# One Trainium2 core, attention into a mixture of experts: first attention's values three units behind its scores, k through VectorE, two weight words converted ahead of chunk 1

## The chip, the cores and the metric

The kernel runs on one core of a Trainium2 chip. TensorE (PE) multiplies matrices, with its weight loads shown apart as PEld; VectorE (DVE), ScalarE (ACT) and GpSimd (POOL) work element by element; SyncE (SP) issues the DMAs. Each engine takes its own instructions strictly in the order in which they are written and waits on semaphores for the others. The metric is the device time of one execution in microseconds (us), as the median of three runs.

## The reference

```
scores = q @ k.T / 8                      # 4 batches, 8 heads, 576 positions, 64 wide
mask: heads 0-3 the last 32 positions; heads 4-7 every 4th of the last 128
attn = exp(scores - max) / (sum + 1e-9);  x = attn @ v   -> 2304 tokens x 512
h = x @ w_in;  x = (h - tanh(h)) @ w_out                 # 512 -> 2048 -> 512
logits = x @ phi                                         # 8 experts x 4 slots
slots  = softmax over tokens(logits).T @ x
slots  = relu(slots[e] @ w1[e]) @ w2[e]  for 8 experts
out    = softmax over slots(logits) @ slots
```

## The kernel before

The mask lets most scores fall away, so the attention of a batch is worked in 12 units, three for each of the four head pairs (in the order `PO`): units 0 to 5 are dilated heads, in 4 blocks of 80 columns, units 6 to 11 are plain ones, in 3 blocks of 96. A unit goes round the engines:

1. **scores** (`emit_scores`): TensorE lays the mask into PSUM (L337) and adds the scores (L359); VectorE takes the largest (L374); ScalarE takes the exponentials and their sums (L377); VectorE adds the epsilon (L389) and inverts (L391); 
2. **norm** (`emit_norm`): GpSimd multiplies by the inverse (L392);
3. **trans** (`emit_trans`): TensorE transposes the weights (L401); ScalarE copies them out of PSUM (L103, `COPY mem<-mm`);
4. **values** (`emit_pv`): TensorE multiplies by v (L422); ScalarE casts the result to its high part (L103, `CAST xhi<-mm`);
5. **low** (`emit_lows`): VectorE subtracts to get the low part (L458).

For each head pair q and k are transposed by TensorE (L308) and taken out of PSUM as `qk` tiles of 128x288: k by a plain copy (L103), q by L316 with the factor 1/8. L103 is the line of the helper `copy`, which runs on the engine that it is told.

The 2048 columns of the hidden layer are 16 **words** of 128 columns. The weights arrive as raw words and are turned into the operands of three fp32r products: `conv_a` (ScalarE, L507), `conv_b` (two VectorE instructions, L515 and L516), then `conv_in_c` (a cast, L103 `CAST wts<-cvb` or `wts<-mem`, and GpSimd's low part, L529). `conv_out_c`, `_d` and `_e` (TensorE L537, L548, L561 and copies by L103) fold the output weights with phi. `emit_h` computes one word for 512 tokens: 4 parts of 3 matmuls (L574 to L576, high by high, low by high, high by low); then tanh (ScalarE, L580), h - tanh h (VectorE, L583) and the logits (L589).

The tokens go in chunks of 512. The order of the program is that of three stages:

- The **first attention** (batch 0) is emitted from a table: `at(t, f, ...)` puts each step of each unit, each conversion and each load at a model time, and the steps are emitted in the order of these times. A unit is 3.45 model us (`ATT0`); `NORM`, `TRANS` and `PV` say how far behind the unit's scores its other steps stand. The weights of words 1 and 2 (`conv_*("in", 0)` and `1`) are converted within it; `emit_h(..., part=range(3))` computes the first three of the four parts of words 1 and 2 at its end (the high parts, as they are called here: "high part 0" and "high part 1"). `warm` matmuls (L205) fill TensorE.
- **Chunk 0** (called chunk 1 where chunks are counted from one) runs as eight **mixed steps** s = 0 to 7 (`mixed_step`), each with words a = 2s and b = 2s + 1, a piece of the attention of batch 1 (`norms`, `trans`, `score`, `values`; masked on VectorE by L371), and the conversions of two words of input and two of output weights for later steps.
- The other chunks run as `phase_step`s, whose weights are all there, then experts and output.

Of the kernel before, what the change touches and what calls it, by code (L numbers as in the profile page):

```python
# [36 lines left out]
    ("out", 0): 0, ("out", 2): 1, ("out", 4): 2, ("in", 0): 3, ("in", 2): 0, ("in", 4): 1, ("out", 6): 2, ("in", 6): 3,  # L37
    ("out", 8): 2, ("out", 10): 1, ("in", 8): 2, ("in", 10): 3, ("out", 14): 2, ("in", 14): 3,
}
ENGS = {'qk': 'AAAA', 'pt': 'AAA', 'hi': 'AAA', 'rem': 'VVA', 'wh': 'VA', 'wt': 'AV', 'wq': 'V', 'wp': 'A'}  # L40
WARM = 5
NWARM = 4
WAT = 0.29
ATT0 = (8.71, 3.45)
NORM = (1.01, 0.28)
TRANS = (2.05, 1.76)
PV = (2.8, 3.39)
QK = (1.54, 1.08)
LQK = (12.33, 21.85)
LV = (4.31, 7.03)  # L50
# [9 lines left out]
LWI = 2.97  # L60
# [4 lines left out]
def moe_kernel(ctx: ExitStack, tc: tile.TileContext, q, k, v, w_in, w_out, phi, w1, w2, out):  # L65
# [8 lines left out]
    NU = 3 * NP  # L74
# [81 lines left out]
    wp = cpart(NFT, NS)  # L156
# [4 lines left out]
    wts, xhi, xlo = {}, {}, {}  # L161
# [340 lines left out]
    def conv_a(kind, ft):  # L502

        f = convs[kind].next()
        hw = raw_t[kind, ft][1].bitcast(F32)

        nc.scalar.activation(out=like(f, kind), in_=hw, func=ACTF.Prelu, scale=2.0 ** -112, alpha=-2.0 ** 32)  # L507
        cvt[kind, ft] = f

    def conv_b(kind, ft):  # L510
        wl, _ = raw_t.pop((kind, ft))
        f = cvt[kind, ft]
        du = f.bitcast(U32)
        dk = like(f, kind).bitcast(U32)
        nc.vector.tensor_scalar(out=du, in0=du, scalar1=3, scalar2=None, op0=ALU.logical_shift_left)  # L515
        nc.vector.scalar_tensor_tensor(  # L516
            out=dk, in0=wl, scalar=29, in1=dk, op0=ALU.logical_shift_right, op1=ALU.bitwise_or
        )
# [4 lines left out]
    def conv_in_c(ft):  # L523
        if ft % 2 == 0:
            wts[ft // 2] = unit("wts", [128, 2, KT, 256], F32R)
        fv = cvt.pop(("in", ft)).rearrange("p (k f) -> p k f", k=KT)
        hi, lo = win(0, ft), win(1, ft)
        copy(ENGS["wh"][ft > 1], hi, fv)
        nc.gpsimd.tensor_tensor(out=lo, in0=fv, in1=hi.bitcast(F32), op=ALU.subtract)  # L529
# [37 lines left out]
    def emit_h(xh, xl, ft, ps=None, part=range(KT)):  # L567

        if ps is None:
            ps = ps_h.tile([128, 512], F32, tag="h", name="h")[:, 0:xh.shape[-1]]  # L570
        for n in part:
            kt = PO[n]
            wh, wl = win(0, ft)[:, kt, :], win(1, ft)[:, kt, :]
            nc.tensor.matmul(ps, lhsT=wh, rhs=xh[:, kt, :], start=(n == 0), stop=False)  # L574
            nc.tensor.matmul(ps, lhsT=wh, rhs=xl[:, kt, :], start=False, stop=False)  # L575
            nc.tensor.matmul(ps, lhsT=wl, rhs=xh[:, kt, :], start=False, stop=(n == KT - 1))  # L576
        return ps

    def emit_tanh(ps, g):
        nc.scalar.activation(out=g, in_=ps, func=ACTF.Tanh)  # L580

    def emit_sub(ps, g):
        nc.vector.tensor_tensor(out=g, in0=ps, in1=g, op=ALU.subtract)  # L583
# [295 lines left out]
    with tc.manual_schedule():  # L879
# [4 lines left out]
        def at(t, f, *args):  # L884
            steps.append((t, len(steps), f, args))

        for b, (t0, dt) in enumerate((ATT0,)):
            for i in range(NU):
                t = t0 + dt * i
                at(t, emit_scores, b, i)  # L890
                at(t + 0.02 * dt, emit_lows)
                at(t + NORM[b] * dt, emit_norm, b, i)
                at(t + TRANS[b] * dt, emit_trans, b, i)
                at(t + PV[b] * dt, emit_pv, b, i)
                if b == 0:
                    at(t + WAT * dt, warm, WARM if i < NWARM else 2)
            for i in range(NU, NU + 3):
                at(t0 + dt * (i + 0.02), emit_lows)
            for p in range(NP):
                for n in range(2):  # L900
                    at(t0 - 0.02 + 0.01 * n if p == 0 else t0 + dt * (3 * p - 3 + n + QK[b]), emit_qk, b, PO[p], n)
                at(t0 + dt * 3 * p - LQK[b], load_qk, b, PO[p])
                at(t0 + dt * 3 * p - LV[b], load_v, b, PO[p], nc.sync)
# [4 lines left out]
        for e in range(KA):  # L908
            t, dt = WO1[0] + WO1[1] * e, WO1[1]
# [3 lines left out]
            at(t + OC * dt, conv_out_c, e)  # L913
            at(t + OD * dt, conv_out_d, e)
            at(t + OE * dt, conv_out_e, e)
        for e in range(2):
            t, dt = WI[0] + WI[1] * e, WI[1]
            at(t - LWI, load_w, "in", e)
            at(t, conv_a, "in", e)
            at(t + CB, conv_b, "in", e)  # L920
            at(t + IC * dt, conv_in_c, e)
        at(45.0, load_w, "in", 2)
        first = []
        for i in range(2):

            at(ATT0[0] + ATT0[1] * (10.65 + 0.5 * i + PV[0]), lambda i: first.append(emit_h(xhi[0], xlo[0], i, part=range(3))), i)
        at(WI[0] + 6.0, scale_q, 1, PO[0])
        for _, _, f, args in sorted(steps, key=lambda s: s[0:2]):
            f(*args)
# [15 lines left out]
        def mixed_step(an, ch, s, xh, xl, gs, posts):  # L945

            a, b = 2 * s, 2 * s + 1
            if s < 5:
                load_w("out", 6 + a)
            if s < 6:  # L950
                load_w("in", 4 + a)
            an.load(*{0: (3, 2), 2: (4, 3), 3: (4, 4)}.get(s, (0, 0)))
            pa, gs[a] = emit_first(ch, xh, xl, a, first), gring.next()
            if s in QKS:
                turn_qk(an.b, PO[QKS.index(s)])
            an.norms(s - 1)
            if s == 0:
                conv_a("in", 2)
                conv_a("in", 3)
            else:  # L960
                for n in (a - 2, a - 1):
                    emit_gT(ch, n, gs[n])
            emit_tanh(pa, gs[a])
            if 0 < s < 7:
                conv_a("in", 2 + a)
                conv_a("in", 2 + b)
            emit_sub(pa, gs[a])
            emit_lows()
            if 0 < s < 6:
                conv_out_c(4 + a)  # L970
                conv_out_c(5 + a)
            if s in (2, 4, 6):
                conv_out_e(3 + a)
            if s < 7:
                conv_b("in", 2 + a)
                conv_in_c(2 + a)
                conv_b("in", 2 + b)
                conv_in_c(2 + b)
            pb, gs[b] = emit_first(ch, xh, xl, b, first), gring.next()
            emit_tanh(pb, gs[b])  # L980
            an.trans(s)
            if 0 < s < 6:
                conv_out_d(4 + a)
                conv_out_d(5 + a)
            emit_sub(pb, gs[b])
            if s < 5:
                conv_a("out", 6 + a)
                conv_a("out", 7 + a)
            an.score(2 * s, 2 * s + 1)
            if s < 5:  # L990
                conv_b("out", 6 + a)
                conv_b("out", 7 + a)
            an.values(s)
            if s + 1 in QKS:
                scale_q(an.b, PO[QKS.index(s + 1)])
            if s:
                emit_logits(ch, a - 1, gs[a - 1])
            emit_logits(ch, a, gs[a])
# [39 lines left out]
        for ch in range(4):  # L1038
# [12 lines left out]
            gs, nxt = {}, None  # L1051
# [29 lines left out]
        for s in range(NFT // 2):  # L1081
            a = 2 * s
# [82 lines left out]
        for a, copy in enumerate((nc.scalar.copy, nc.vector.tensor_copy)):  # L1165
            ps = mm([128, 2, 32])
            for c in range(2):
                dt = 2 * a + c
# [87 lines left out]
```

## Time and profile before

| | |
|---|---|
| median of 3 runs | 454.63 us (453.74 to 455.15) |
| the profiled execution | 453.27 us, of which the span shown is 451.3 us |
| PE, DVE, ACT, POOL busy | 92%, 56%, 45%, 19% of the span |
| TensorE's granted clock | 0.985 of full speed in the mean |

The page cuts the span in 40 slices of 11.3 us. The first attention lies in the first five, the mixed steps in slices 6 to 13, the rest in the others. In the slices of the rest TensorE shows a 9 (90% or more) until the output begins. "Idle before" is what an engine stood still ahead of an instruction, with the event that released it. Times of the trace are from the span's start.

### The profile page before, as it was taken

The page shows a single profiled execution, that of the slowest core. Times are in us where ns is not written, and L with a number is a line of the kernel's source. Part 1 is how long each engine was busy: PE and PEld are TensorE (multiplying, and loading weights), DVE is VectorE, ACT ScalarE, POOL GpSimd, SP SyncE. Part 2 cuts the span into 40 slices and gives each one's busy share as a digit, 9 for nine tenths or more (in the row PEclk, how much of TensorE's full clock was granted, in tenths as well). Part 3 has the DMA queues.
Part 4 walks back from the last instruction along what each step waited for, and adds up shares of the span by engine and source line. Part 5 has one row for each costly group of instructions (what it writes and reads, how often), then busy time and mean ns, then how long its engine had stood idle before and what let it go on. Part 6 is the DMA issues. An engine that isn't in the chain of part 4 may idle for free.

```text
span 451.3 us, 11351 instructions
## 1 busy us (share of the span) xinstructions
PE 415.8 (92%) x4555; PEld 305.0 (68%) x4555; DVE 253.0 (56%) x617; ACT 204.9 (45%) x701; POOL 84.2 (19%) x99
## 2 busy tenths in 40 slices
PE   6988888999898999999999999999999999999980
PEld 4766656877776768787776777776777689555330
DVE  0465759999974757864768765536444331333051
ACT  4787547777773455554271745221121122213040
POOL 3231444334334130314031311000000000010000
PEclk9999999899999999999999999999999999999997
DMA  8988898989657013414503302192005599899928
GB/s 232 252 222 263 247 174 235 257 257 309 199 93 137 4 26 70 81 23 88 97 2 60 71 6 95 45 415 102 0 1 169 180 391 407 329 409 406 403 120 312
DMA packets 102021, 81.16 MB, mean 180 GB/s; under 512 B 78032, under 2 KB 81872, under 8 KB 101968
## 3 DMA queue, kind: packets, MB, share of 16 engines
q1 hardware_dynamic: 101968, 80.43, 59.3%
q8 instruction: 36, 0.59, 0.6%
q14 instruction: 17, 0.14, 0.1%
HBM read 71.50 MB, written 8.91 MB: 178 GB/s over the span
## 4 chain that ended last, share of the span: by engine, by line
PE 53%; issue 13%; DVE 12%; ACT 11%; DMA 5%; SPq 2%; POOL 0%; ACTq 0%; POOLq 0%; DVEq 0%
PE h L574 9%; PE h L575 8%; PE h L576 8%; ACT mem L377 6%; PE mm L359 4%; PE h L797 3%; PE lg L589 3%; PE y L822 3%; PE mm L713 3%; PE mm L422 3%; DMA rqk<-in_q_dram 2%; DMA rqk<-in_k_dram 2%; PE mm L401 2%; DVE gt L596 2%; SPq L241 2%
## 5 line engine op out<-in xcount | busy, mean ns | idle before, releaser
L574 PE MATMUL h<-xhi,wts 128*128 128x512 f32 x256 | 106.2, 415 | 1.1 <-ACT wts L103 1.1
L576 PE MATMUL h<-xhi,wts 128*128 128x512 f32 x256 | 101.1, 395 | 0.8 <-POOL wts L529 0.8
L575 PE MATMUL h<-xlo,wts 128*128 128x512 f32 x256 | 100.9, 394 | 0.0
L580 ACT ACTIVATE mem<-h 128x512 f32<-128x512 f32 x72 | 42.9, 596 | 117.2 <-PE h L576 109.6
L583 DVE TENSOR_TENSOR mem<-h,mem 128x512 f32<-128x512 f32 x72 | 49.2, 683 | 74.1 <-ACT mem L580 74.0
L392 POOL TENSOR_TENSOR mem<-mem 128x320 f32<-128x320 f32 (+1 forms) x48 | 33.1, 700 | 164.3 <-DVE mem L391 108.1
L574 PEld LDWEIGHTS h<-xhi,wts 128*128 128x128 f32 x256 | 48.9, 191 | 16.9 <-issue 6.1
L576 PEld LDWEIGHTS h<-xhi,wts 128*128 128x128 f32 x256 | 48.7, 190 | 12.2 <-POOL wts L529 1.2
L575 PEld LDWEIGHTS h<-xlo,wts 128*128 128x128 f32 x256 | 48.7, 190 | 8.7
L377 ACT ACTIVATE mem<-mem 128x80 f32<-128x80 f32 (+1 forms) x126 | 44.6, 356 | 17.3 <-DVE mem L374 17.3
L596 DVE STREAM_TRANSPOSE gt<-mem 128x512 f32<-128x512 f32 x64 | 41.0, 683 | 0.0
L422 PE MATMUL mm<-mem,v 80*64 80x48 f32 (+1 forms) x672 | 26.2, 226 | 10.4 <-ACT mem L103 10.4
L422 PEld LDWEIGHTS mm<-mem,v 80*64 80x64 f32 (+1 forms) x672 | 22.2, 137 | 16.0 <-ACT mem L103 14.3
L103 ACT COPY mem<-mm 96x384 f32<-96x384 f32 (+4 forms) x64 | 25.4, 428 | 6.0 <-PE mm L401 4.9
L359 PE MATMUL mm<-qk 64*64 64x96 f32 (+2 forms) x672 | 25.1, 247 | 2.5 <-DVE cvb L103 1.8
L589 PE MATMUL lg<-mem 128*32 128x128 f32 x576 | 26.3, 283 | 0.9 <-DVE mem L583 0.9
L359 PEld LDWEIGHTS mm<-qk 64*64 64x64 f32 (+1 forms) x672 | 18.9, 134 | 9.2 <-DVE cvb L103 2.6
L377 ACT ACTIVATION_READ_ACCUMULATOR mem<-mem 128x1 f32 x126 | 23.8, 189 | 0.0
L401 PE MATMUL mm<-mem 112*80 112x112 f32 (+1 forms) x168 | 23.1, 270 | 0.1
L589 PEld LDWEIGHTS lg<-mem 128*32 128x32 f32 x576 | 15.1, 110 | 11.7 <-issue 9.0
L250 POOL TENSOR_SCALAR rqk<-rqk 128x576 f32<-128x576 f32 x12 | 19.7, 1648 | 0.0
L401 PEld LDWEIGHTS mm<-mem 112*80 112x80 f32 (+1 forms) x168 | 16.3, 122 | 4.9 <-issue 2.0
(178 smaller groups left out, 618.7 us busy)
## 6 DMA issues: line engine op xcount, KB each, us to landing
ex<-in_moe_w_dram SPq DMA_DIRECT2D x21, 1024.0 KB, 10.9
gt<-in_moe_w_out_dram SPq DMA_DIRECT2D x7, 1024.0 KB, 8.0
gt<-in_moe_w_in_dram SPq DMA_DIRECT2D x7, 1024.0 KB, 7.8
gt<-in_moe_w_dram SPq DMA_DIRECT2D x6, 1024.0 KB, 10.6
mem<-in_moe_w_dram SPq DMA_DIRECT2D x5, 1024.0 KB, 7.7
wo_dram<-cva SPq DMA_DIRECT2D x16, 256.0 KB, 5.6
wo<-wo_dram SPq DMA_DIRECT2D x4, 1024.0 KB, 7.6
out_dram<-o SPq DMA_DIRECT2D x8, 512.0 KB, 4.8
```

The costliest lines, as they stand in the source:

```text
L359: nc.tensor.matmul(ps[64 * y:64 * y + nr, c, :], lhsT=qT[b, p][r, q0:q0 + step * (nr - 1) + 1:step], rhs=kT[b, p][r, k0:k0 + step * (nk - ...
L377: nc.scalar.activation(out=pr[:, c, :], in_=ps[:, c, :], func=ACTF.Exp, bias=nm[:, c:c + 1], accum_out=sm[:, c:c + 1],)
L392: nc.gpsimd.tensor_tensor(out=pr, in0=pr, in1=rc.unsqueeze(2).to_broadcast([128, nb, nk]), op=ALU.mult)
L401: nc.tensor.transpose(ps[:, c, :], pr[0:P, c, :], ident[0:P, 0:P])
L422: nc.tensor.matmul(o[64 * hh:64 * hh + 64, col:col + nq], lhsT=vt[b, p](n, hh), rhs=pt[:, c, 64 * (x ^ sw):64 * (x ^ sw) + nq], start=True ...
L574: nc.tensor.matmul(ps, lhsT=wh, rhs=xh[:, kt, :], start=(n == 0), stop=False)
L575: nc.tensor.matmul(ps, lhsT=wh, rhs=xl[:, kt, :], start=False, stop=False)
L576: nc.tensor.matmul(ps, lhsT=wl, rhs=xh[:, kt, :], start=False, stop=(n == KT - 1))
L580: nc.scalar.activation(out=g, in_=ps, func=ACTF.Tanh)
L583: nc.vector.tensor_tensor(out=g, in0=ps, in1=g, op=ALU.subtract)
L589: nc.tensor.matmul(lgs[ch][32 * j:32 * j + 32, 0:128], lhsT=wp[:, ft, :], rhs=g[:, 128 * j:128 * j + 128], start=(ft == 0), stop=(ft == NF ...
L596: nc.vector.transpose(out=gt[:, ft, :], in_=g)
```

## The change

Four things are written in another order, and one eviction changes its engine.

- `ENGS['qk']` goes from `AAAA` to `VVAA`: the two k copies of each head pair are VectorE's instead of ScalarE's. q stays with ScalarE.
- `PV` goes from 2.8 to 3.15 units behind the scores: the values of unit i stand behind scores and trans of later units, not ahead of them. For the last three units the distance is 2.95, 2.5 and 1.9; for the last two transposes it is 1.9 and 1.3 units. The low parts stand just ahead of each unit's scores, not just behind.
- Words 3 and 4 (`"in"`, 2 and 3) are converted in the table, no longer in mixed step 0, so that their casts precede both tanh's of the step.
- High parts 0 and 1 stand at 12.6 and 13.0 units, not at 13.45 and 13.95.
- In mixed steps 1 to 6 tanh and subtraction of word b and the transposes are emitted ahead of the casts of the next step's words, and `conv_out_d` ahead of the second word's `conv_b`.

```diff
-ENGS = {'qk': 'AAAA', 'pt': 'AAA', ...
+ENGS = {'qk': 'VVAA', 'pt': 'AAA', ...
-TRANS = (2.05, 1.76)
-PV = (2.8, 3.39)
+TRANS = [2.05] * 10 + [1.9, 1.3]
+PV = [3.15] * 9 + [2.95, 2.5, 1.9]
...
+                at(t - 0.01, emit_lows)
                 at(t, emit_scores, b, i)
-                at(t + 0.02 * dt, emit_lows)
...
-        for e in range(2):
+        for e in range(4):
             t, dt = WI[0] + WI[1] * e, WI[1]
-            at(t - LWI, load_w, "in", e)
+            at(t - LWI if e < 2 else 45.0, load_w, "in", e)
...
-            at(ATT0[0] + ATT0[1] * (10.65 + 0.5 * i + PV[0]), lambda i: first.append(emit_h(xhi[0], xlo[0], i, part=range(3))), i)
+            at(ATT0[0] + ATT0[1] * (12.6 + 0.4 * i), lambda i: first.append(emit_h(xhi[0], xlo[0], i, part=range(3))), i)
...
-            if s == 0:
-                conv_a("in", 2)
-                conv_a("in", 3)
-            else:
+            if s:
...
-            if s < 7:
+            if 0 < s < 7:
                 conv_b("in", 2 + a)
-                conv_in_c(2 + a)
-                conv_b("in", 2 + b)
-                conv_in_c(2 + b)
             pb, gs[b] = emit_first(ch, xh, xl, b, first), gring.next()
             emit_tanh(pb, gs[b])
+            emit_sub(pb, gs[b])
             an.trans(s)
+            if 0 < s < 7:
+                conv_in_c(2 + a)
             if 0 < s < 6:
                 conv_out_d(4 + a)
                 conv_out_d(5 + a)
-            emit_sub(pb, gs[b])
+            if 0 < s < 7:
+                conv_b("in", 2 + b)
+                conv_in_c(2 + b)
```

TensorE's instructions in the first attention, around the values of unit 6 (L422; a minus is the order of before, a plus the new one):

```order
 L537 MATMUL mm<-mem,cva 128x128 x4
-L422 MATMUL mm<-mem,v 64x64 x6
 L337 LDWEIGHTS mem
 L337 MATMUL mm<-mem 128x288
 L359 MATMUL mm<-qk 64x96 x6
 L401 MATMUL mm<-mem 96x128 x3
+L422 MATMUL mm<-mem,v 64x64 x6
```

The values have moved from ahead of a later unit's mask and scores to behind them and behind a transpose.

ScalarE's instructions at the end of the attention (L507 is `conv_a`, `CAST wts` the casts of words 3 and 4, L580 the tanh's of words 1 and 2):

```order
-L507 ACTIVATE cvb<-gt 128x512
-L507 ACTIVATE mem<-gt 128x512
-L580 ACTIVATE mem<-h 128x512
-L103 CAST wts<-cvb 128x4x128
-L103 CAST wts<-mem 128x4x128
-L580 ACTIVATE mem<-h 128x512
+L507 ACTIVATE cvb<-gt 128x512
+L103 CAST xhi<-mm 128x3x48
+L103 CAST wts<-cvb 128x4x128
+L507 ACTIVATE mem<-gt 128x512
+L103 CAST wts<-mem 128x4x128
+L580 ACTIVATE mem<-h 128x512 x2
```

Both casts now precede both tanh's, and word 3's `conv_a` precedes the last high part of the values.

ScalarE's instructions at the end of mixed step 2 (L580 is the tanh of word b, `COPY mem<-mm` the transposed weights for the values):

```order
 L103 COPY cvb<-mm 128x512
 L103 COPY mem<-mm 128x128
-L103 CAST wts<-cvb 128x4x128
-L103 CAST wts<-mem 128x4x128
-L580 ACTIVATE mem<-h 128x512
-L103 COPY mem<-mm 80x448 x2
+L580 ACTIVATE mem<-h 128x512
+L103 COPY mem<-mm 80x448 x2
+L103 CAST wts<-cvb 128x4x128
+L103 CAST wts<-mem 128x4x128
 L507 ACTIVATE cva<-gt 128x512 x2
```

The tanh and the copies have moved from behind the two casts to ahead of them.

## Rows read from the trace of the kernel before

**Rows 1.** Windows: busy us of PE, PEld, DVE, ACT, POOL; PEclk, DMA share, GB/s.
```profile
20.00:30.00 10.00, 7.54 (x117) 6.17 (x119) 4.97 (x15) 8.03 (x32) 3.92 (x9) 1.00 0.97 237
...
90.00:100.00 10.00, 10.00 (x132) 8.27 (x133) 9.13 (x23) 8.36 (x31) 3.25 (x4) 1.00 0.86 231
...
140.00:155.00 15.00, 15.00 (x120) 11.14 (x120) 9.10 (x21) 4.07 (x14) 0.90 (x1) 1.00 0.39 67
```

**Rows 2.** Timeline of unit 3 (start, us, engine, line; idle before, releaser).
```profile
17.30 0.31 PE L337 MATMUL mm<-mem 64*128 64x320 bf16 x1
...
20.16 0.52 ACT L103 COPY mem<-mm 80x448 f32<-80x448 f32 x1
...
20.74 0.67 PE L422 MATMUL mm<-mem,v 80*64 80x48 f32 x16 [0.84 <-ACT mem L103]
...
21.34 0.31 PE L337 MATMUL mm<-mem 64*128 64x320 bf16 x1
```

**Rows 3.** Waits in the first attention, 8 to 57 us (total, times, longest).
```profile
PE mm L422 <- ACT mem L103: 6.1, 10, 1.4
```

**Rows 4.** Groups by shape, 8 to 57 us, ScalarE (busy, mean ns, idle before).
```profile
L103 ACT COPY qk<-mm 128x288 f32<-128x288 f32 x6 | 3.3, 655 | 0.0
...
L103 ACT COPY mem<-mm 128x128 f32<-128x128 f32 x1 | 0.3, 266 | 0.7 <-PE mm L561 0.7
```

**Rows 5.** The same of VectorE.
```profile
L103 DVE COPY cvb<-mm 128x512 f32<-128x512 f32 x3 | 2.0, 680 | 0.0
...
L103 DVE COPY cvb<-mm 128x128 f32<-128x128 f32 x5 | 1.4, 285 | 0.1
```

**Rows 6.** Timeline of TensorE from unit 11 to high part 0.
```profile
48.00 0.29 PE L337 MATMUL mm<-mem 64*128 64x288 bf16 x1
...
52.99 0.98 PE L561 MATMUL mm<-mem,cvb 128*128 128x32 f32 x8
...
54.75 0.53 PE L401 MATMUL mm<-mem 128*96 128x128 f32 x3
55.04 0.48 PE L574 MATMUL h<-xhi,wts 128*128 128x512 f32 x1
...
57.29 0.57 PE L422 MATMUL mm<-mem,v 96*64 96x64 f32 x12
```

**Rows 7.** Timeline of all engines from unit 11's values into mixed step 0.
```profile
58.34 0.30 DVE L458 TENSOR_TENSOR xlo<-mm,xhi 128x144 fp32r<-128x144 f32 x1
...
60.55 0.29 DVE L103 COPY cvb<-mm 128x128 f32<-128x128 f32 x1 [1.91 <-PE mm L548]
...
62.69 0.41 DVE L515 TENSOR_SCALAR cvb<-cvb 128x512 uint32<-128x512 uint32 x1
...
64.52 0.50 PE L574 MATMUL h<-xhi,wts 128*128 128x512 f32 x1 [1.11 <-ACT wts L103]
...
66.06 0.69 DVE L583 TENSOR_TENSOR mem<-h,mem 128x512 f32<-128x512 f32 x1 [1.18 <-ACT mem L580]
66.07 0.80 PE L576 MATMUL h<-xhi,wts 128*128 128x512 f32 x1 [0.81 <-POOL wts L529]
...
66.67 0.48 DVE L371 TENSOR_TENSOR mem<-mm,mem 128x320 f32<-128x320 f32 x1
```

**Rows 8.** Timeline of VectorE at the ends of mixed steps 0 and 4.
```profile
78.08 0.69 DVE L583 TENSOR_TENSOR mem<-h,mem 128x512 f32<-128x512 f32 x1 [0.78 <-ACT mem L580]
78.69 0.48 DVE L371 TENSOR_TENSOR mem<-mm,mem 128x320 f32<-128x320 f32 x1
...
126.85 0.45 DVE L371 TENSOR_TENSOR mem<-mm,mem 128x288 f32<-128x288 f32 x1
```

**Rows 9.** Timeline of TensorE, values of mixed step 6.
```profile
136.87 0.95 PE L422 MATMUL mm<-mem,v 96*64 96x64 f32 x24 [1.47 <-ACT mem L103]
```

**Rows 10.** Windows around the lower clock at 66 us (columns of Rows 1).
```profile
62.40:65.80 3.40, 1.75 (x42) 0.94 (x38) 2.42 (x5) 1.50 (x3) 1.25 (x1) 1.00 0.83 176
65.80:69.20 3.40, 3.13 (x7) 2.49 (x8) 3.03 (x7) 2.88 (x11) 3.07 (x3) 0.50 1.20 161
```

More of the change, by code (lines that the diff above doesn't have):

```diff
@@ L39 @@
 }
-ENGS = {'qk': 'AAAA', 'pt': 'AAA', 'hi': 'AAA', 'rem': 'VVA', 'wh': 'VA', 'wt': 'AV', 'wq': 'V', 'wp': 'A'}
+ENGS = {'qk': 'VVAA', 'pt': 'AAA', 'hi': 'AAA', 'rem': 'VVA', 'wh': 'VA', 'wt': 'AV', 'wq': 'V', 'wp': 'A'}
 WARM = 5
@@ L889, in moe_kernel @@
                 t = t0 + dt * i
+                at(t - 0.01, emit_lows)
                 at(t, emit_scores, b, i)
-                at(t + 0.02 * dt, emit_lows)
                 at(t + NORM[b] * dt, emit_norm, b, i)
-                at(t + TRANS[b] * dt, emit_trans, b, i)
-                at(t + PV[b] * dt, emit_pv, b, i)
+                at(t + TRANS[i] * dt, emit_trans, b, i)
+                at(t + PV[i] * dt, emit_pv, b, i)
                 if b == 0:
                     at(t + WAT * dt, warm, WARM if i < NWARM else 2)
-            for i in range(NU, NU + 3):
-                at(t0 + dt * (i + 0.02), emit_lows)
+            for i in (NU, NU + 0.55, NU + 0.95):
+                at(t0 + dt * i, emit_lows)
             for p in range(NP):
@@ L921, in moe_kernel @@
             at(t + IC * dt, conv_in_c, e)
-        at(45.0, load_w, "in", 2)
         first = []
         for i in range(2):
-            at(ATT0[0] + ATT0[1] * (10.65 + 0.5 * i + PV[0]), lambda i: first.append(emit_h(xhi[0], xlo[0], i, part=range(3))), i)
+            at(ATT0[0] + ATT0[1] * (12.6 + 0.4 * i), lambda i: first.append(emit_h(xhi[0], xlo[0], i, part=range(3))), i)
         at(WI[0] + 6.0, scale_q, 1, PO[0])
```

## The prediction

> **What bounds the kernel now.** I read the page's slices first, then windows, then the waits, then the timeline engine by engine. From the end of the mixed steps on TensorE is busy without a gap: 15.00 of 15 us between 140 and 155 us [rows 1], and a 9 in the slices after it until the output. Work that reaches that point earlier should end earlier by as much, so I look for what changes before 140 us.
>
> In the first attention no engine is full: between 20 and 30 us TensorE has 7.54 of 10 us, ScalarE 8.03, VectorE 4.97 [rows 1]. It is a loop over engines. Unit 3's scores begin at 17.30; its exponentials occupy ScalarE until 20.16, where the copy of unit 1's transposed weights runs; TensorE, after 0.84 us of idling for that copy, multiplies unit 1's values at 20.74, and only behind them, at 21.34, come unit 4's mask and scores [rows 2]. So the next scores wait for a copy that waits for this unit's exponentials. The wait comes up 10 times and costs 6.1 us [rows 3], 0.61 a unit. From unit 3 (17.30) to unit 11 (48.00) [rows 2, 6] eight periods take 30.70 us, 3.84 each.
>
> In the mixed steps the order round word b is what matters: at the end of step 0 VectorE idles 0.78 us for the tanh of word b [rows 8], and the masked maxima of batch 1 (L371) begin behind it. That tanh stands in ScalarE's queue behind both casts, and these wait for VectorE's conversions. The same idle stands at five step ends (0.78 to 0.96). From the first L371, in step 0 at 66.67, to the one at 126.85 [rows 7, 8] five such periods take 60.18 us. In step 6 TensorE waits 1.47 us at the values for the copy that stands behind the same casts [rows 9].
>
> **The change part by part.**
>
> *Values behind the scores.* The wait of 0.61 us a unit need not vanish: the copy still takes ScalarE's time, only TensorE does the next scores in front of it. Lower end of a period: TensorE's own 7.54 tenths of 3.84, 2.9 us [rows 1]. Upper end: 3.84, if another link of the loop is as long. The nearest reading is 3.84 less the wait, 3.23; I take 3.4, since the values that no longer wait must still be waited for somewhere by the casts behind them. Eight periods give 8 x 0.44 = 3.5 us at unit 11's scores (0 to 7.5 by the two ends).
>
> *k on VectorE.* Six copies of 655 ns in this stretch leave ScalarE [rows 4], 2 in three units, 0.44 us a unit. No row shows VectorE at 128x288 with this layout. From its copies out of PSUM, 285 ns at 128 columns and 680 at 512 [rows 5], a straight line gives 450 ns at 288; the other end is ScalarE's 655. I take 450, the same engine's. VectorE is half idle there [rows 1], so I charge nothing; what it costs if the copy stands ahead of a maximum is in the first rival.
>
> ScalarE's own copy at 128 columns takes 266 ns, VectorE's 285 [rows 4, 5]. The Trainium skill (Perfetto Trace Analysis, Optimizing Scalar/DVE Operations) speaks against the move: it puts the access overhead to PSUM at about 125 ns for VectorE and 51 for ScalarE. By the page eight copies would cost 8 x 74 ns, 0.6 us more engine time in all as an estimate; the rows at equal shape show a quarter of that difference, and for the tile itself the other sign. The sum goes by the rows.
>
> *The end of the attention.* Here time is given back. Before, unit 11's transposes (54.75) stood directly ahead of high part 0 (55.04) [rows 6]. Now the product L561 (0.98 us) and unit 10's values (0.57, as unit 11's at 57.29) stand between [rows 6]: 1.5 us. And unit 11's maximum and inverse have the low parts of earlier units, and word 2's conversion, ahead of them on VectorE; four more pieces at the 0.30 us of a low part [rows 7] are 1.2 us. High part 0 then comes 3.5 - 1.5 - 1.2 = 0.8 us earlier. I take 0.6, the end of the chain being ScalarE's, which is fuller than TensorE (2.7 later to 4.8 earlier by the two ends). Everything behind it up to unit 11's values keeps its order.
>
> *Words 3 and 4.* From unit 11's values (57.29) to the first L371 (66.67) are 9.38 us [rows 6, 7]. In it VectorE idled 1.91 us ahead of 60.55 and 1.18 us for the second tanh at 66.06; between 62.69 and 66.06 it did the two conversions, TensorE waiting 1.11 us for word 3's cast and 0.81 for word 4's low part [rows 7]. Now the conversions start while VectorE idled and the subtractions follow the transposes directly. The conversions cannot be hidden whole: word 4's `conv_a` stands behind word 3's cast, that behind word 3's `conv_b`, and both tanh's stand behind word 4's cast. At most the 3.37 us between 62.69 and 66.06 go, at least nothing (the tanh of word 1 waits for a cast as the tanh of word 2 did). Those 1.18 us at the tanh are the wait that goes; half of them I leave to the hand-overs of that chain: 0.7 us earlier. Front of the mixed steps: 0.6 + 0.7 = 1.3 us.
>
> *Word b before the casts, steps 1 to 5.* The 0.78 us goes from each step in which VectorE's chain is the pace. Where TensorE is full the step cannot shorten by it: 10.00 of 10 us between 90 and 100 [rows 1] covers two of the five ends. So 3 x 0.78 = 2.3 us; ends: 0 (VectorE, 9.13 of 10 there, is itself the pace) and 5 x 0.78 = 3.9.
>
> *Step 6.* The copies now stand ahead of the casts. Of TensorE's 1.47 us [rows 9] I leave 0.6, about what a unit's wait for its copy was in the attention [rows 3]: 0.9 us (0 to 1.47). SP's and POOL's instructions keep their order; loads behind 70 us are gated by conversions and move with them.
>
> Sum: 1.3 + 2.3 + 0.9 = 4.5 us, from the profiled execution's 453.27 to 448.8. That execution is 1.36 us under the median of the runs shown, 454.63; the same 4.5 from the median give 450.1.
>
> **The rivals.**
>
> *VectorE becomes the bound (slower).* k copies and low parts now stand in its queue ahead of a unit's maximum, and ScalarE's exponentials wait for that. Per unit: two copies in three units at 655 ns, 0.44, and a low part of 0.30 [rows 4, 7], 0.74 against 0.61 saved: 0.13 x 8 = 1.0 us later at unit 11. It decides from the point where the two together exceed 0.61 us. With 2.7 more at the attention's end, no gain in steps whose pace VectorE sets, 0.9 in step 6 and 0.7 from words 3 and 4: 3.7 - 1.6 = 2.1 later, 456.7. For it: VectorE is at 9.13 of 10 in the steps. Against: in the attention it is at half [rows 1], so most copies should find it idle.
>
> *The clock drops at the attention's end.* After a stretch with TensorE at 1.75 of 3.40 us the granted clock was 0.50 (1.2 GHz) for 3.40 us [rows 10]; a matmul then takes twice as long, which costs 1.7 us. With the values waiting for inverse, norm and transpose of the last units with nothing else queued, a new gap of that kind can stand near 50 us. One such drop there, and the attention's 0.6 gone: 450.1 + 1.7 + 0.6 = 452.4. For it: the gap in TensorE's work that the new tail makes. Against: the drop at 66 us came after the two waits for words 3 and 4, and these go, which may give 1.7 us back.
>
> *Transfers hold the pace.* The DMA share is 0.97 between 20 and 30 us and 0.86 from 90 to 100 [rows 1]. If q, k and raw words arrive no earlier, the attention and the first steps cannot move up, and what stays is step 6 and a little of the later steps: 454.63 - 0.9 - 0.4 = 453.3. For it: the queues are never long empty. Against: no wait for a DMA is on the list of waits between 8 and 57 us [rows 3].
>
> **How the numbers follow.** A measurement of this kernel tells 0.3%, 1.36 us, from no change: faster is under 453.27, slower above 455.99. Forecast (448 to 452 as its own range): 0.58, all of it faster. More than forecast, with the drop at 66 us gone too, counts in it: 448.4. The clock at the attention's end: 0.18, a sixth of it within 0.3%. Transfers: 0.12, half of it within. VectorE: 0.12, 0.09 slower and 0.03 within. Faster 0.58 + 0.15 + 0.06, from which I take 0.04 for what I have no row for, is 0.75; within 0.15; slower 0.10. The range for 8 in 10 goes from 446.5 (the drop gone and all of the 3.9 us) to 454.8, which leaves out the slower end of VectorE's case and what lies below.
>
> **What the changed profile would show.** Right: unit 3 to unit 11's scores in about 27 us, the row of waits from L422 to the copy well under 6.1 us; L371 of batch 1 near 65.4; no wait of word 3's or 4's first matmul for a cast or low part; VectorE's idling for L580 at step ends gone; TensorE's wait at step 6's values near 0.6. Wrong: maxima that VectorE begins late behind copies of `qk`; a clock of 0.5 around 50 us; step periods that stay at 12 us although the wait for the tanh is gone, with another wait in its place; or an end that moves less than the L371 of step 5.

## The result and the profile after

The changed kernel is slower: 460.29 us in the median of 4 runs (459.47 to 461.71) against 454.19 (452.72 to 455.15), a ratio of 1.0141 (95%: 1.0102 to 1.018). Here and below a few executions of some kernels are slow ones at a lower mean clock; the ratios leave them out, the medians do not. The profiled execution has a span of 458.2 us, 6.9 more than before's 451.3.

The middle of the attention did what was forecast in kind. TensorE's wait for the copy ahead of the values, 6.1 us in ten times before [rows 3], is off the list of waits; unit 3's scores begin at 15.88 and unit 11's at 45.62, eight periods of 3.72 us against 3.84 [rows 2, 6]. These eight periods give 1.0 us; the other 1.4 of the 2.4 us by which unit 11's scores are early are there at unit 3 already (15.88 against 17.30). From unit 11's scores on time is lost. TensorE's timeline of the end (start, us, line, shapes; idle before and its releaser):

```profile
15.88 0.31 PE L337 MATMUL mm<-mem 64*128 64x320 bf16 x1
...
45.62 0.29 PE L337 MATMUL mm<-mem 64*128 64x288 bf16 x1
...
51.51 0.88 PE L401 MATMUL mm<-mem 128*96 128x128 f32 x3 [3.10 <-POOL mem L392]
...
55.35 0.87 PE L401 MATMUL mm<-mem 128*96 128x128 f32 x3 [1.08 <-POOL mem L392]
56.02 1.75 PE L561 MATMUL mm<-mem,cvb 128*128 128x32 f32 x8
57.70 0.91 PE L422 MATMUL mm<-mem,v 96*64 96x64 f32 x12
58.54 0.80 PE L574 MATMUL h<-xhi,wts 128*128 128x512 f32 x1
...
62.40 0.57 PE L422 MATMUL mm<-mem,v 96*64 96x64 f32 x12
```

Unit 11's scores are early, but TensorE then waits 3.10 us for GpSimd's norm of unit 10 and 1.08 for that of unit 11. Unit 10's norm needs an inverse (L391, at 50.47) that stands in VectorE's queue behind unit 11's maximum (L374, at 49.31 in the next rows). High part 0 begins at 58.54 against 55.04, unit 11's values at 62.40 against 57.29 [rows 6]. Windows of the same stretch (PE, PEld, DVE, ACT, POOL; granted clock, DMA share, GB/s) show the clock at 0.50, its lower level of 1.2 GHz, from 53.60 to 60.40 and for part of the window ahead of it; the row of L561 reads 1.75 us there, where it read 0.98 at full clock [rows 6]:

```profile
50.20:53.60 3.40, 2.09 (x17) 1.61 (x18) 1.97 (x7) 2.64 (x11) 0.81 (x2) 0.61 0.93 297
53.60:57.00 3.40, 2.32 (x13) 1.90 (x11) 1.58 (x6) 0.53 (x2) 2.39 (x3) 0.50 1.12 326
57.00:60.40 3.40, 3.40 (x20) 2.86 (x20) 0.49 (x3) 1.20 (x4) 1.14 (x1) 0.50 0.50 71
...
87.60:91.00 3.40, 3.40 (x17) 3.01 (x16) 3.40 (x10) 2.54 (x7) 1.40 (x2) 0.63 0.76 214
```

Then VectorE, at unit 11's maximum (L374), from unit 11's values to the first L371, and at the ends of steps 1 and 5 (the two ends in [rows 8], called those of steps 0 and 4 in the prediction, are steps 1 and 5 as the kernel counts):

```profile
47.39 0.43 DVE L515 TENSOR_SCALAR cvb<-cvb 128x512 uint32<-128x512 uint32 x1 [2.05 <-ACT cvb L507]
...
49.31 0.45 DVE L374 TENSOR_REDUCE mem<-mm 128x3 f32<-128x288 f32 x1
...
63.45 0.29 DVE L458 TENSOR_TENSOR xlo<-mm,xhi 128x144 fp32r<-128x144 f32 x1
63.66 0.41 DVE L515 TENSOR_SCALAR cvb<-cvb 128x512 uint32<-128x512 uint32 x1
...
70.48 0.47 DVE L371 TENSOR_TENSOR mem<-mm,mem 128x320 f32<-128x320 f32 x1
...
79.32 0.68 DVE L583 TENSOR_TENSOR mem<-h,mem 128x512 f32<-128x512 f32 x1
...
80.32 1.38 DVE L515 TENSOR_SCALAR mem<-mem 128x512 uint32<-128x512 uint32 x1
...
136.48 0.45 DVE L371 TENSOR_TENSOR mem<-mm,mem 128x288 f32<-128x288 f32 x1
```

The first L371 is at 70.48 against 66.67 [rows 7], 3.8 us late. Word b's L583 no longer waits 0.78 us as in [rows 8] (79.32), but the conversion behind it takes 1.38 us in its first instruction, where L515 took 0.41 at 62.69 [rows 7]; from the first L371 to 136.48 the five periods take 66.00 us, before 60.18. ScalarE, GpSimd and TensorE beside it, and TensorE at step 6's values:

```profile
82.45 0.62 ACT L103 CAST wts<-mem 128x512 fp32r<-128x512 f32 x1 [2.39 <-DVE mem L516]
...
80.14 1.27 POOL L529 TENSOR_TENSOR wts<-cvb,wts 128x512 fp32r<-128x512 f32 x1 [2.64 <-ACT wts L103]
...
84.42 1.82 POOL L250 TENSOR_SCALAR rqk<-rqk 128x576 f32<-128x576 f32 x1
...
85.95 0.63 PE L537 MATMUL mm<-mem,cva 128*128 128x128 f32 x4 [1.17 <-DVE cva L516]
87.39 0.63 PE L537 MATMUL mm<-mem,cva 128*128 128x128 f32 x4 [0.82 <-DVE cva L516]
...
143.31 0.95 PE L422 MATMUL mm<-mem,v 96*64 96x64 f32 x24 [0.49 <-ACT mem L103]
...
146.00 0.50 PE L576 MATMUL h<-xhi,wts 128*128 128x512 f32 x1 [0.51 <-POOL wts L529]
```

The second cast waits 2.39 us for that conversion; L529 and L250 of GpSimd run beside VectorE's conversions; TensorE stands twice, 1.17 and 0.82 us, for the output conversions (L537 behind VectorE's `cva`), and from 88 us the clock is down again (0.63 in the last window above). The trace of before has such a stretch in the steps too, from about 79.4 to 82.8. The wait at step 6's values did fall as forecast, from 1.47 [rows 9] to 0.49 us, but behind it TensorE now waits 0.51 us for a low part (L529, at 146.00).

L371 is VectorE's, and the kernel's time goes by TensorE. There unit 11's values are 5.1 us late (62.40 against 57.29) and step 6's values 6.4 us (143.31 against 136.87 [rows 9]), near the 6.9 us of the whole span. So in this trace most of the loss is there at the end of the attention, and the 5.8 us by which VectorE's five periods are longer overstate what the steps cost.

### The profile page after: what moved, and what is told of

Same layout as the page of the kernel before. It is cut to its first block, busy times and chain, and to the rows that moved or that the text cites. A ratio compares the mean times of both kernels' runs of the same rounds, so it can differ in the third digit from the quotient of the medians.

```text
span 458.2 us, 11352 instructions
## 1 busy us (share of the span) xinstructions
PE 420.3 (92%) x4555; PEld 306.5 (67%) x4555; DVE 264.6 (58%) x625; ACT 200.1 (44%) x693; POOL 83.5 (18%) x99
## 4 chain that ended last, share of the span: by engine, by line
PE 68%; DVE 14%; ACT 7%; DMA 4%; issue 2%; SPq 2%; POOL 1%; DVEq 0%; POOLq 0%; ACTq 0%
PE h L574 12%; PE h L576 11%; PE h L575 11%; PE mm L713 4%; PE lg L589 4%; ACT mem L377 3%; PE mm L359 3%; PE h L797 3%; PE mm L422 3%; PE y L822 3%; PE mm L401 3%; PE warm L205 2%; SPq L243 2%; DMA wo<-wo_dram 1%; DVE cva L516 1%
## 5 line engine op out<-in xcount | busy, mean ns | idle before, releaser
L580 ACT ACTIVATE mem<-h 128x512 f32<-128x512 f32 x72 | 43.0, 599 | 120.1 <-PE h L576 112.6
L583 DVE TENSOR_TENSOR mem<-h,mem 128x512 f32<-128x512 f32 x72 | 49.0, 681 | 68.5 <-ACT mem L580 68.5
L103 ACT COPY mem<-mm 80x448 f32<-80x448 f32 (+4 forms) x64 | 25.5, 430 | 9.0 <-PE mm L401 7.8
L359 PE MATMUL mm<-qk 64*64 64x96 f32 (+2 forms) x672 | 23.5, 246 | 5.0 <-ACT qk L316 2.6
L422 PE MATMUL mm<-mem,v 80*64 80x48 f32 (+1 forms) x672 | 26.8, 229 | 1.0 <-ACT mem L103 1.0
L422 PEld LDWEIGHTS mm<-mem,v 80*64 80x64 f32 (+1 forms) x672 | 22.8, 140 | 5.5 <-ACT mem L103 1.7
L359 PEld LDWEIGHTS mm<-qk 64*64 64x64 f32 (+1 forms) x672 | 18.0, 133 | 10.9 <-issue 4.7
L377 ACT ACTIVATE mem<-mm,mem 128x80 f32<-128x80 f32 (+1 forms) x42 | 13.5, 331 | 15.6 <-DVE mem L389 9.6
```

Source lines behind the costliest of these rows:

```text
L359: nc.tensor.matmul(ps[64 * y:64 * y + nr, c, :], lhsT=qT[b, p][r, q0:q0 + step * (nr - 1) + 1:step], rhs=kT[b, p][r, k0:k0 + step * (nk - ...
L377: nc.scalar.activation(out=pr[:, c, :], in_=ps[:, c, :], func=ACTF.Exp, bias=nm[:, c:c + 1], accum_out=sm[:, c:c + 1],)
L422: nc.tensor.matmul(o[64 * hh:64 * hh + 64, col:col + nq], lhsT=vt[b, p](n, hh), rhs=pt[:, c, 64 * (x ^ sw):64 * (x ^ sw) + nq], start=True ...
```

## The experiments

All times are medians; ratios are against the kernel before, run beside each.

**1. The steps' order alone.** Before, with the new order in mixed steps 1 to 6 only (step 0 as it was).

> The kernel before, with only the new order of mixed steps 1 to 6 (tanh and subtraction of word b, then transposes, then the casts; the second word's conv_b behind conv_out_d). Theory S, the steps' order costs by itself: VectorE's first conversion instruction of word b now falls together with GpSimd's low part of word a and takes 1.4 us instead of 0.42, ScalarE holds the second cast for it, and the output conversions come late; five steps then end 2 to 4 us later: 456.5 to 458.5. Theory F, the loss lies in the attention's end alone and the steps only pass it on: the wait of 0.78 us at word b's tanh goes and the time falls by 1 to 3 us, 451.5 to 453.5.

457.46 us, ratio 1.0052 (1.0022 to 1.0081): theory S. The first L371 is at 66.35, as before; the loss is behind it. ScalarE, GpSimd, VectorE and TensorE at the end of step 3, then a row of the waits from 64 to 140 us (total, times, longest):

```profile
104.52 0.62 ACT L103 CAST wts<-mem 128x512 fp32r<-128x512 f32 x1 [2.39 <-DVE mem L516]
...
102.20 1.27 POOL L529 TENSOR_TENSOR wts<-cvb,wts 128x512 fp32r<-128x512 f32 x1 [3.94 <-ACT wts L103]
...
106.48 1.82 POOL L250 TENSOR_SCALAR rqk<-rqk 128x576 f32<-128x576 f32 x1
...
102.39 1.37 DVE L515 TENSOR_SCALAR mem<-mem 128x512 uint32<-128x512 uint32 x1
...
106.83 1.03 DVE L516 SCALAR_TENSOR_TENSOR cva<-raww,cva 128x512 uint32<-128x512 uint32 x1
...
108.01 0.63 PE L537 MATMUL mm<-mem,cva 128*128 128x128 f32 x4 [1.49 <-DVE cva L516]
...
PE mm L537 <- DVE cva L516: 5.6, 7, 1.5
```

L515 of word b starts 0.19 us behind L529 and ends within 0.3 us of it: 1.37 us. L250, later than before because L529 of word b is, stretches the output conversion too (L516 1.03 us), and TensorE waits 1.49 us for that. Such waits come to 5.6 us in seven times; in the trace of before there is one, of 0.5 us.

**2. The steps' order undone.** The changed kernel with before's order in the steps.

> The changed kernel with the order of before in mixed steps 1 to 6; k on VectorE, the attention's table and words 3 and 4 ahead of the tanh's stay. Theory S: about 2.6 us of the 6 go, 457 to 458, the first L371 near 70.5 as in the changed kernel. Theory F: nothing goes, 460; or the steps get worse, 461 to 463.

459.95 us (456.0 to 460.95), ratio 1.0077 (1.0037 to 1.0117): the front alone costs about half. First L371 at 71.10; the five periods from there to 132.57 take 61.5 us, near before's. Theory S by the ratio, though its interval just overlaps the changed kernel's; the median would have left it open.

**3. The attention's table alone.**

```diff
+TRANS = [2.05] * 10 + [1.9, 1.3]
+PV = [3.15] * 9 + [2.95, 2.5, 1.9]
... low parts and high parts as in the change, nothing else
```

> The kernel before with only the attention's table changed (values, transposes, low parts and first high parts at their new places); k stays with ScalarE, words 3 and 4 in mixed step 0, the steps in the old order. Theory E, the end of the attention is where the front is lost (late inverse, two waits of TensorE for the norm, half clock from 51 to 61 us): high part 0 near 58 to 59 instead of 55.0, time 457 to 460. Theory K, the loss comes from k copies and low parts in VectorE's queue: without k on VectorE the loss goes to at most 1 us, 454 to 455.

458.96 us, ratio 1.0081 (1.0047 to 1.0115): theory E, with k still on ScalarE. With experiment 1, 0.81% and 0.52% make 1.33% of the change's 1.41%. The parts do not simply add, though: words 3 and 4, 0.8% faster alone (experiment 13), are in the change too, and with table and k (experiment 2, 0.77%) next to nothing of their gain is left by the ratios.

```profile
55.06 0.87 PE L401 MATMUL mm<-mem 128*96 128x128 f32 x3 [1.08 <-POOL mem L392]
...
58.25 0.80 PE L574 MATMUL h<-xhi,wts 128*128 128x512 f32 x1
...
61.90 0.57 PE L422 MATMUL mm<-mem,v 96*64 96x64 f32 x12
```

The same end as in the changed kernel, within 0.5 us in each row.

**4. k alone on VectorE.** `'qk': 'VVAA'`.

> The kernel before with only the k copies moved to VectorE. Theories S and E: no change beyond 0.7 us, 453.5 to 455; the copies take 0.45 to 0.65 us each. Theory K: maxima start behind the copies and the attention ends 1 us or more later, 455.5 or more.

454.46 us, ratio 0.9989 (0.9961 to 1.0018): no change. The price was off all the same. VectorE's group by shape in the changed kernel, 8 to 57 us (busy, mean ns, idle before):

```profile
L103 DVE COPY qk<-mm 128x288 f32<-128x288 f32 x6 | 3.4, 634 | 1.6 <-PE mm L308 1.6
```

634 ns, not 450: the layout costs VectorE what it cost ScalarE (655) [rows 4].

**5. GpSimd's low parts left out.** Experiment 1 without L529 for words 5 to 16; the third product takes the high part.

```diff
+        if ft < 4:
+            nc.gpsimd.tensor_tensor(out=lo, in0=fv, ...)
```

> The kernel before with the new order of the mixed steps, in which GpSimd's low parts of the weights (L529) of words 5 to 16 are left out and the third product takes the high part instead, so that TensorE's work is the same. Theory P, GpSimd's instructions beside VectorE's conversions are what the new order costs: L515 of word b goes back from 1.38 to 0.42 us, and half or more of the 2.4 us by which the new order is slower goes; 454 to 456. Theory Q, the order itself costs (word b's conversion and the cast that waits for it stand ahead of the next output conversions): L515 is short but the steps stay long and the time stays at 456.5 to 458.

449.71 us, ratio 0.9898 (0.9849 to 0.9946), 1.5% under experiment 1, some 7 us: theory P, and more than the loss. TensorE's waits for the output conversions fall from 5.6 us to 1.3. VectorE and ScalarE at the end of step 1:

```profile
76.44 0.42 DVE L515 TENSOR_SCALAR mem<-mem 128x512 uint32<-128x512 uint32 x1
...
77.61 0.62 ACT L103 CAST wts<-mem 128x512 fp32r<-128x512 f32 x1 [1.44 <-DVE mem L516]
```

L515 takes 0.42 us again. Without GpSimd's low parts the new order shows no loss. What the old order would gain from leaving them out was not run.

**6. Both conversions ahead of the tanh.**

```diff
                 conv_b("in", 2 + a)
+                conv_b("in", 2 + b)
...
                 conv_in_c(2 + a)
+                conv_in_c(2 + b)
...
-                conv_b("in", 2 + b)
-                conv_in_c(2 + b)
```

> The kernel before with the new order of mixed steps 1 to 6 but for one thing: the second word's conv_b stands where it stood before, directly behind the first word's, ahead of word b's tanh; tanh, subtraction and transposes still precede both casts. Theory Q: ScalarE's wait of 2.4 us for the second cast goes, the output conversions come as early as before or earlier, and the time is that of before or up to 2 us less, 452.5 to 454.7. Theory P: GpSimd's low parts now run beside the output conversions (L515 and L516 of cva) in every step, and 1 us or more of the loss stays, 455.5 to 457.5.

450.13 us, ratio 0.9916 (0.9886 to 0.9946): faster than before, by twice what theory Q allowed at most. ScalarE's long wait for the second cast is gone, as Q had it (its longest is 0.4 us); the loss of 1 us or more that theory P forecast for this order did not come. Steps 1 and 5 by VectorE and GpSimd:

```profile
66.85 0.48 DVE L371 TENSOR_TENSOR mem<-mm,mem 128x320 f32<-128x320 f32 x1
...
75.95 0.42 DVE L515 TENSOR_SCALAR mem<-mem 128x512 uint32<-128x512 uint32 x1
...
77.02 0.68 DVE L583 TENSOR_TENSOR mem<-h,mem 128x512 f32<-128x512 f32 x1
...
78.01 0.48 DVE L371 TENSOR_TENSOR mem<-mm,mem 128x320 f32<-128x320 f32 x1
...
76.77 1.46 POOL L529 TENSOR_TENSOR wts<-cvb,wts 128x512 fp32r<-128x512 f32 x1 [2.65 <-ACT wts L103]
...
123.61 0.45 DVE L371 TENSOR_TENSOR mem<-mm,mem 128x288 f32<-128x288 f32 x1
```

L515 runs in 0.42 us before L529 begins, word b's L583 follows the conversion without a wait, and five periods take 56.76 us. L529 now runs beside L371, which reads 0.48 us as in [rows 8].

**7. One cast between.** Before, with word b's tanh ahead of the second cast alone.

> The kernel before with a smaller move in mixed steps 1 to 6: word b's tanh stands ahead of the second cast alone, all the rest as before. The prediction's reason (VectorE's 0.78 us wait for that tanh is on the path): the wait goes, GpSimd's low parts move by half a microsecond only, and 1 to 3 us are gained, 452 to 453.7. Theory P and Q allow that; that the wait was not on the path at all (TensorE full, or the next conversions late anyway) gives no change, 454 to 455.5.

455.21 us, ratio 1.0007 (0.9971 to 1.0044): no change. From 68.91 to 129.28 the five periods take 60.37 us. The wait turned into another:

```profile
PE mm L359 <- ACT mem L103: 4.8, 4, 1.9
```

So VectorE's 0.78 us at the tanh are not worth 0.78 us on their own: the copies of the transposed weights still stood behind a cast, and TensorE's scores now waited for them, where before its values had (3.9 us between 64 and 140 us before, 0.9 now).

**8. Filling ahead of the last transposes.** Experiment 3 with 20 matmuls (L205) ahead of unit 10's transposes and 10 ahead of unit 11's.

> The kernel with the attention's table alone changed, plus 20 filling matmuls ahead of unit 10's transposes and 10 ahead of unit 11's, where TensorE waited 3.1 and 1.1 us for the norms. Theory C, half of the 3.7 us lost there is the lower clock from 51 to 61 us: the clock stays at 1.00 there, unit 11's transposes come at the same time as without filling (55.0 to 55.6), high part 0 near 56.7 instead of 58.3, unit 11's values 2 to 3 us earlier, time 456 to 457.5. Theory L, it is only the late inverse and what now stands behind unit 11's transposes: the clock changes little on the path, time 458 to 460.

456.69 us, ratio 1.0058 (1.0024 to 1.0092), overlapping experiment 3's interval. The clock stays at 1.00 up to 57 us and falls then, 0.55 from 57.0 to 60.4:

```profile
55.13 0.53 PE L401 MATMUL mm<-mem 128*96 128x128 f32 x3 [0.90 <-POOL mem L392]
...
56.91 0.50 PE L574 MATMUL h<-xhi,wts 128*128 128x512 f32 x1
...
61.09 0.57 PE L422 MATMUL mm<-mem,v 96*64 96x64 f32 x12
```

High part 0 comes 1.3 us earlier than in experiment 3, unit 11's values 0.8: a part of theory C, no more.

**9. High part 0 directly behind unit 11's transposes.** Experiment 3 with the first high part at 12.31 units.

> The kernel with the attention's table alone changed, in which the nine matmuls of high part 0 stand directly behind unit 11's transposes, as before, ahead of L561 and unit 10's values. If 1.5 us of the loss are what stands between those transposes and high part 0, high part 0 starts 0.4 us behind the transposes instead of 3.2 and unit 11's values come up to 1 us earlier than that kernel's 61.9; if unit 10's values, moved behind, are what everything waits for, unit 11's values stay near 61.9.

A single run, 457.92 us, so its time says little. It ran 1.06 us later than experiment 3 up to there (transposes at 56.12 against 55.06), and unit 11's values came at 61.64, so 1.3 us sooner by that measure.

**10. The middle alone.** `PV = [3.15] * 8 + [2.8] * 4`, transposes, low and high parts as before.

> The kernel before with the values of units 0 to 7 behind the scores three units on, as in the changed kernel, but units 8 to 11, the last transposes, the low parts and the first high parts where they were before. Theory E (the last units' order is what loses the front): unit 11's scores come 1.5 to 2.5 us earlier as in the changed kernel, TensorE's wait of 3.1 us for unit 10's norm is gone and high part 0 comes no later than before's 55.0 us; time 452.5 to 454.5. Theory V (values behind the scores cost by themselves, whatever the end): 455.5 or more.

457.24 us, ratio 1.005 (1.0002 to 1.0098). The ten runs lie in two clusters, 453.5 to 454.8 and 459.7 to 460.7; the trace is one of the lower, and what the others do no trace shows. Not theory E, whose earlier scores do not come; theory V's range holds the median, but only half of the runs. TensorE's transposes wait for the low parts:

```profile
26.10 0.55 PE L401 MATMUL mm<-mem 112*80 112x112 f32 x4 [1.35 <-DVE xlo L458]
...
48.66 0.29 PE L337 MATMUL mm<-mem 64*128 64x288 bf16 x1
```

Unit 11's scores come at 48.66, no earlier than before's 48.00. By these rows the values gain only if the low parts move with them, as in the change, where they stand ahead of the maxima.

**11. The changed kernel with both conversions ahead,** as in experiment 6.

> The changed kernel with one thing moved: in mixed steps 1 to 6 the second word's conv_b directly behind the first word's, ahead of word b's tanh. If the loss in the steps is that one move (GpSimd's low part beside VectorE's conversion, the cast that waits for it, the output conversions that come late), some 6 us of the changed kernel's time go, as between the steps' order alone (457.5) and this order on the kernel before (450.1): 453 to 455. If the attention's late end spoils the steps by itself, less than 3 us go: 457 to 459.

451.68 us, ratio 0.9953 (0.993 to 0.9976): the change is now faster than before, by the place of one word's conversion (1.9% between the two ratios, some 8.6 us). Its first L371 is still at 70.94.

**12. Experiments 6 and 10 together.**

> The kernel before with two parts: values of units 0 to 7 behind the scores three units on (the last units as before), and in mixed steps 1 to 6 tanh, subtraction and transposes of word b ahead of both casts, with both conv_b ahead of the tanh. If the two add up: 448 to 450, below 450.1 by what the first alone gives. If the attention's gain is lost again at its end: 449.5 to 451.

450.94 us, ratio 0.9912 (0.988 to 0.9944): what experiment 6 gives alone.

**13. Words 3 and 4 alone in the table.**

> The kernel before with only words 3 and 4 converted in the attention's table, so that their casts precede both tanh's. If the prediction's step on these words holds by itself, the first L371 comes 0.7 to 1.3 us earlier than before's 66.7 and the time falls by about 1 us, 453 to 454.3; if both tanh's now wait for the second cast as long as the second one did before, nothing changes, 454 to 455.5.

451.97 us, ratio 0.9918 (0.9873 to 0.9962): faster, and by more than expected. From unit 11's values (60.59, after a stretch at the lower clock in this execution) to the first L371 (66.64) are 6.05 us, 9.38 before. VectorE:

```profile
57.03 0.43 DVE L515 TENSOR_SCALAR cvb<-cvb 128x512 uint32<-128x512 uint32 x1
...
61.64 0.30 DVE L458 TENSOR_TENSOR xlo<-mm,xhi 128x144 fp32r<-128x144 f32 x1
...
66.64 0.48 DVE L371 TENSOR_TENSOR mem<-mm,mem 128x320 f32<-128x320 f32 x1
```

Word 3's conversion (57.03) is done before unit 11's low part (61.64). In the changed kernel it stands behind it (63.45, then 63.66), because the last low part was moved up; there the stretch takes 8.08 us. No run moved that low part back, so that it is the reason is read from the rows and not shown.

**14. Words 3 and 4 with both conversions ahead.** Experiments 6 and 13.

> The kernel before with words 3 and 4 in the table and the mended order of the mixed steps (both conv_b ahead of word b's tanh, casts behind it). If words 3 and 4 add to what the mended order gives by itself (0.84% in its own run): 448.5 to 450; if they add nothing: 450 to 451.

444.66 us (444.03 to 448.59), ratio 0.9782 (0.973 to 0.9835): the fastest of all, below both kernels, with before's attention. The profiled execution has no stretch at the lower clock before 140 us:

```profile
56.94 0.57 PE L422 MATMUL mm<-mem,v 96*64 96x64 f32 x12
...
62.99 0.48 DVE L371 TENSOR_TENSOR mem<-mm,mem 128x320 f32<-128x320 f32 x1
...
118.67 0.43 DVE L371 TENSOR_TENSOR mem<-mm,mem 128x288 f32<-128x288 f32 x1
```

First L371 3.7 us earlier than before's, five periods of 55.68 us in all. Experiments 6 and 13 add up to 1.66% by their ratios and this is 2.18%; how much of it is the clock that did not fall is not separated.

**15. The changed kernel, mended:** experiments 8, 9 and 11 together.

> The changed kernel with the mended order of the mixed steps and with both repairs of the attention's end that moved unit 11's values earlier one by one: filling matmuls ahead of the last two transposes, and high part 0 directly behind unit 11's transposes. If the clock and the order behind those transposes are what the front lost, unit 11's values come near 59.5 instead of 62.9 and the time is 449 to 450.5, below the 451.7 without the repairs; if the late inverse is all, 451 to 452.

448.77 us, ratio 0.9857 (0.9817 to 0.9897). Unit 11's values at 58.93, near the 59.5 expected and 3.9 us before those of experiment 11 (0.6 of it is there at unit 11's scores); first L371 at 67.02. So clock and order behind the transposes were most of the loss at the end, and the attention's new order is still no gain against experiment 14's old one.

## Why the prediction was wrong

Two steps failed, by about as much each.

*Word b before the casts, steps 1 to 5* (forecast 2.3 us earlier, ends 0 to 3.9): the steps' order alone costs 0.52%, 2.4 us. The working put no cost on word b's conversion at its new place, and its worst end was no gain; it did not ask what runs beside the conversion on another engine. GpSimd's order was indeed the same, as the prediction says, but its low part of word a now fell onto VectorE's conversion of word b (0.42 to 1.4 us), the second cast waited for that, L529 and L250 fell onto the output conversions, and TensorE waited for those. Experiments 5, 6 and 11 show it. That the lower clock behind these waits is a part of the loss is not shown, as the steps of before have such a stretch too.

L515 begun beside L529 lasts until 0.3 us behind L529's end (102.39 + 1.37 against 102.20 + 1.27), while L371, which takes one operand from PSUM, keeps its 0.48 us beside it. The trace of before had the sign already, at an output conversion beside L250:

```profile
79.25 1.65 POOL L250 TENSOR_SCALAR rqk<-rqk 128x576 f32<-128x576 f32 x1
...
80.53 0.65 DVE L515 TENSOR_SCALAR cva<-cva 128x512 uint32<-128x512 uint32 x1
```

There L515 takes 0.65 us in place of 0.42 and again ends 0.3 us behind GpSimd's instruction. The Trainium skill (SBUF — State Buffer, Who interferes with whom) has a rule that would have warned: VectorE in its two-port modes and GpSimd contend for one shared pair of ports, which the one that issues first holds for its whole instruction while the other stands still. The rows of L515 above agree with it; that L515 takes its operands in such a mode, no row shows by itself. L516's 1.03 us beside L250 end ahead of L250 (106.83 + 1.03 against 106.48 + 1.82) and are not explained by it.

With the conversion kept ahead five periods take 56.8 us, 3.4 less than before, inside the ends of this step, but that is luck: the 0.78 us at the tanh, the term that the sum was made of, bring nothing by themselves (experiment 7), and the copies behind the casts are a part of the gain. Two readings in this step were wrong as well: four ends of five wait for the tanh, 0.78 or 0.79 us (the 0.96 of the fifth is a wait for L548, ahead of the copies before it), and the window from 90 to 100 us holds one end, not two.

*The end of the attention* (forecast 0.6 us earlier, ends 2.7 later to 4.8 earlier) was 3.5 us later at high part 0 and 5.1 at unit 11's values; the table alone costs 0.81%, 3.7 us. Three terms were off. The eight periods gave 1.0 us, not 3.5. The sum then carried that gain through to high part 0, but unit 11's maximum hardly profited, 49.31 us against 49.59, since word 1's conversion stands ahead of it on VectorE and waits 2.05 us for ScalarE (47.39); unit 10's norm follows from there, and unit 11's inverse comes 0.8 us later than before (54.29 against 53.52), behind word 2's conversion and low parts as the working had it. The third is the clock.

By the rows unit 11's transposes are 0.6 us late (55.35 against 54.75); high part 0 begins 3.2 us behind them, 0.3 before, with L561 and unit 10's values between (1.5 us by the prediction, 2.7 at the lower clock); unit 11's values follow 3.9 us behind it, 2.3 before, with one product more (L548) and most of it at the lower clock. The second rival had the mechanism and the place, near 50 us, but one drop of 3.40 us for 1.7 us [rows 10]; the windows show it down from 51 to 61 us. Experiments 8, 9 and 15 bring back most of it. How it divides between clock and order is not settled: filling alone only delayed the drop. That the drop belongs to the new order is likely but not certain: the clock fell at 50 to 52 us in all five traces with the new table and no filling, and with before's order of the attention in two of eight (experiments 7 and 13), at 54 to 55.

*Values behind the scores* removed the wait as said, but the periods are 3.72 us, not 3.4. What grew in its place are TensorE's waits for q (L359 behind L316, up to 1.35 us, 2.6 in all, 0.5 before) and ScalarE's for L389 (9.6 us in all, 5.2 before); that these took the gain no run shows by itself.

*Words 3 and 4* was right in sign: 0.7 forecast, 1.3 in the changed kernel (9.38 to 8.08), 3.3 alone, against the bound of 3.37. What hid two thirds was, by the rows, the place of the last low part. *k*: right in worth (nothing), wrong in price. *Step 6*: the wait fell by 0.98 us against 0.9, and 0.51 of it came back in the wait at 146.00. The range's lower end, 446.5, would be 446.8 by its own terms.

The first rival had the right engine, VectorE, for the steps, and the wrong reason: not k in its queue (experiment 4), but its neighbour. The low parts in its queue were never run apart, so their share at the attention's end is open. For the third, transfers, nothing was found: experiments 1 and 6 move the time both ways with no load changed.

## What to carry to other kernels

When an instruction is moved past others, lay the timelines of all engines side by side at its new place: its duration in the old trace holds only for its old company. A wait on an engine that is nearly full is seldom worth its length; look for what takes its place (experiment 7) before it goes into a sum. Test the parts of a change apart: here two of four cost 6 us together (experiments 1 and 3), one was worth nothing and one, with the other mended, is the best kernel, 2.2% under before.

## What was not expected of the hardware

VectorE's L515 (uint32, 128x512) takes 0.42 us alone, 1.06 to 1.52 begun beside GpSimd's L529 in the changed kernel, each time until 0.3 us behind L529's end, and 0.80 beside L250; L371, which reads PSUM, takes 0.48 us beside the same L529. And the granted clock fell in the attention's end of some executions whose program is the same up to there: from about 54 to 60.6 us in experiment 13's and not at all in experiment 14's.
